# Linear attention feeding a gelu MLP: token quarters in the first group, a later load of k, and batch 2's transposes moved to the crossbar

## The chip, the cores and the metric

The kernel runs on one core of a Trainium2 chip. The metric is the device time of one execution in microseconds (us), as the median of several runs. Times in this document are of that kind unless they are said to be from the profile, which is one execution recorded by the hardware profiler.

The engines are named as the profile names them: PE (TensorE, matrix multiplies, PEld its weight loads), ACT (ScalarE), DVE (VectorE), POOL (GpSimd) and SP (SyncE, which here only issues transfers). Each takes its instructions in the order of the program. DMA stands for the transfers between the memories.

## The reference

```python
def phi(x):
    return np.where(x > 0, x, np.exp(x) - 1.0) + 1.0
q_p, k_p = (phi(q), phi(k))
kv = np.einsum('bhsd,bhse->bhde', k_p, v)
z = np.sum(k_p, axis=2)
num = np.einsum('bhsd,bhde->bhse', q_p, kv)
den = np.einsum('bhsd,bhd->bhs', q_p, z)[..., None] + 1e-06
attn = num / den                                       # 8 batches, 8 heads, 576 tokens, 64 wide
x = attn.transpose(0, 2, 1, 3).reshape(4608, 512)
h = x @ w_in                                           # 512 x 2048
g = 0.5 * h * (1.0 + np.tanh(sqrt(2 / pi) * (h + 0.044715 * h**3)))
out = g @ w_out                                        # 2048 x 512
```

All inputs and the output are float32 in HBM.

## The kernel before

Each batch has 576 tokens: 512 "main" tokens in four chunks of 128, and 64 "rest" tokens. The rests of all batches, 512 tokens, are the ninth group. A group j has a first half (h = x times w_in in 16 blocks of 128 hidden columns, `first_half`, a gelu on each block on ACT) and a second half (16 slots of four matmuls with w_out, `second_half`). The groups run one after the other, and the attention of a later batch is laid between the blocks and slots: `at(ph, j, slot, fn)` hangs a piece of work behind block or slot `slot` of half `ph` of group j. So `(2, 1, 7)` is "second half of group 1, after slot 7". The order of instructions on every engine is the order in which this program writes them.

The attention of a batch is: exps on ACT (`exp_main`; they need another function table than gelu, so a table load stands before and after), phi on DVE (`phi_of`, a line and a minimum), v cast to bf16 on DVE (`cast_v`), the transpose of q (`qt`), kv on PE (`kv_mm`, evacuated by `kv_evac`), the numerator and denominator per chunk on PE (`nab_mm` into n_ps), their quotient x on DVE (`nab_evac`), and the transpose of x into `xts[b]`, which is the right operand of the first half. A transpose is either four PE matmuls against an identity and a copy (`pe_tx`), or one crossbar DMA (`dma_start_transpose`) in SP's queue. Before the change batches 0, 1 and 2 take PE for x, and batches 3 to 7 the crossbar.

SP's queue holds all loads of k, q, v and the weights, and all crossbar transposes. POOL's queue loads the rests. Loads go through six buffers (`pld`), each 1 MB. PSUM has four one-bank buffers (`ps_ho`, for h_ps, o_ps and some transposes) and two two-bank buffers (`ps_a`, for kv, n_ps, transposes, and the wide h_ps of blocks 12 to 15 of groups 0 and 1 and of blocks 4 to 7 of group 0). Some h blocks are begun early on half of their tokens (`first_mm_early`) while the last chunks of x are still being made. For a pair of batches, `plan_rest` transposes the rest's q (`qtr`) and makes its x for `xt_rest`.

Group 0 starts while the weights are still loading: w_in comes in four blocks and w_out in four, each cast to bf16 by POOL (one half of w_out's last by ACT).

Of the kernel before, what the change touches and what calls it, by code (L numbers as in the profile page):

```python
# [8 lines left out]
FP32 = mybir.dt.float32  # L9
# [6 lines left out]
def kernel(  # L16
# [12 lines left out]
    nc = tc.nc  # L29
# [45 lines left out]
    def load_rest_half(src, t, m, s, eng):  # L75
        eng.dma_start(
            out=t[REST * s : REST * (s + 1)],
            in_=src[2 * m + s, :, MAIN:S, :].rearrange("h p d -> p h d"),
        )
# [36 lines left out]
    load_rest_half(k, ld["kr", 0], 0, 0, nc.sync)  # L116
    load_rest_half(v, ld["vr", 0], 0, 0, nc.sync)
    ld["v", 0] = load_main(v, 0, "v_x", nc.sync, parts=2)
    w_st = [load_w_in(0), load_w_in(1, None, slice(0, 256))]
    ld["k", 1] = load_main(k, 1, "k_x", nc.sync)  # L120
    load_rest_half(k, ld["kr", 0], 0, 1, nc.sync)
    load_w_in(1, w_st[1], slice(256, 512))


    ident = const.tile([P, P], BF16, name="ident")
# [244 lines left out]
            kv_mm(0, 2 * h + i, kv_ps, i)  # L370
        kv_evac(0, kv_ps[:, 0:1], h, nc.scalar.copy)
    keep_warm(1)
    for i in range(2):
        cast_w_in_halves(i)
    x_c = []

# [23 lines left out]
    nab0(2)  # L400
    keep_warm(1)
    tx0(1)
    ke1 = exp_main("k", 1)
    kre1 = pe.tile([P, 1, H, D], BF16, name="kr_e")
    exp_rest_half("kr", kre1, 1)
    gelu_table()
    nab0(3)
    tx0(2)
    first_mm_early(0, 0)
    first_mm_early(0, 1)  # L410
    tx0(3)
    first_mm_early(0, 2)
    first_mm_early(0, 3)


    for i in (2, 3):
        w_st.append(load_w_in(i))
        cast_w_in_halves(i)
    phi["k", 1] = phi_of(ld["k", 1], ke1, "k_p")
    phi_rest_half("kr", kre1, 1)  # L420
    wo_st = [load_w_out(0)]
    ld["q", 1] = load_main(q, 1, "q_x", nc.sync, parts=2)
    wo_st += [load_w_out(i) for i in (1, 2)]
    load_rest_half(v, ld["vr", 0], 0, 1, nc.sync)
    ld["v", 1] = load_main(v, 1, "v_x", nc.sync)
    wo_st.append(load_w_out(3))
# [47 lines left out]
            at(*qr_at, lambda: box["qr"]())  # L474
        at(*table_at, gelu_table)

    def plan_attention(b, ph, j, s_kv, s_n):

        box = {}

        def kv(i):
            if i == 0:
                box["kv"] = ps_a.tile([P, 2, 512], FP32, name="kv_ps", tag="a")
            kv_mm(b, i, box["kv"])

        for i in range(NP):
            at(ph, j, s_kv[i], lambda i=i: kv(i))
        at(ph, j, s_kv[3], lambda: kv_evac(b, box["kv"]))

        def nab(c):  # L490
            n_ps = ps_a.tile([P, 2, 512], FP32, name="n_ps", tag="a")
            nab_mm(qts[b][:, c], kvbds[b % 4], n_ps)
            box["x", c] = nab_evac(n_ps)

        def tx(c):
            if c == 0:
                xts[b] = pt.tile([P, NP, MAIN], BF16, name="xt")
            nc.sync.dma_start_transpose(
                out=xts[b][:, :, P * c : P * (c + 1)],
                in_=box["x", c].rearrange("p a t d -> p (a t d)"),  # L500
            )

        for c in range(C):
            at(ph, j, s_n[c], lambda c=c: nab(c))
            at(ph, j, s_n[c], lambda c=c: tx(c))

    def plan_rest(m, j0, j1):
        box = {}
# [21 lines left out]
    def plan_second():  # L530

        b = 1
        box = {}

        def exps():
            box["q"] = pe.tile([P, C, H, D], BF16, name="q_e")
            for s in halves:
                exp_into(box["q"], ld["q", b], s)
            gelu_table()

        def phis():
            phi["q", b] = pphi.tile([P, C, H, D], BF16, name="q_p")
            for s in halves:
                phi_line(phi["q", b], ld["q", b], s)
                phi_min(phi["q", b], box["q"], s)

        def cast_vs():
            cast_vr(0, (1,))
            cast_v(b, nc.vector.tensor_copy)

        def last_w_out():
            cast_w_out_halves(3, (nc.gpsimd.tensor_copy, nc.scalar.copy))
            load_rests(1, (("kr", k), ("vr", v)))
            for s in range(2):
                load_rest_half(q, ld["qr", 0], 0, s, nc.gpsimd)
            load_rests(1, (("qr", q),))

        def kv():
            kv_ps = ps_a.tile([P, 2, 512], FP32, name="kv_ps", tag="a")
            for i in range(NP):  # L560
                kv_mm(b, i, kv_ps)
            kv_evac(b, kv_ps)

        def tq(h):
            if h == 0:
                box["qt"] = pt.tile([P, C, NP, P], BF16, name="qt")
            t_ps = ps_a.tile([P, 4, NP, P], BF16, name="t_ps", tag="a")
            t_q(q_src(b), None, 2 * h, 2, t_ps)
            copy = nc.vector.tensor_copy if h else nc.scalar.copy
            copy(out=box["qt"][:, 2 * h : 2 * h + 2], in_=t_ps[:, 0:2])  # L570

        def nab(c):
            n_ps = ps_a.tile([P, 2, 512], FP32, name="n_ps", tag="a")
            nab_mm(box["qt"][:, c], kvbds[b], n_ps)
            box["x", c] = nab_evac(n_ps)

        def tx(c):
            copy = nc.scalar.copy if c < 2 else nc.vector.tensor_copy
            pe_tx(b, c, box["x", c], c < 2, copy)

        def early(m):
            first_mm_early(1, m)

        at(1, 0, 11, exps)
        at(2, 0, 0, phis)
        at(2, 0, 0, cast_vs)
        for fn, c, slot in (
            (tq, 0, 7), (tq, 1, 7), (lambda c: kv(), 0, 10), (lambda c: last_w_out(), 0, 10),
            (nab, 0, 11), (nab, 1, 12), (nab, 2, 13), (tx, 0, 13), (nab, 3, 14),
            (tx, 1, 14), (tx, 2, 15), (early, 0, 15), (early, 1, 15), (tx, 3, 15),  # L590
            (early, 2, 15),
        ):
            at(2, 0, slot, lambda fn=fn, c=c: fn(c))

    def plan_third():

        b = 2
        box = {}

        def exps():  # L600
            box["k"] = exp_main("k", b)
            box["kr"] = phi_rest("kr", 1)
            box["q"] = exp_main("q", b)
            box["qr"] = phi_rest("qr", 0)
            gelu_table()

        def phis(n):
            phi[n, b] = phi_of(ld[n, b], box[n], n + "_p")

        def cast_vs():  # L610
            cast_v(b, nc.vector.tensor_copy)
            cast_vr(1)

        def qtr():
            qts[b] = pt.tile([P, C, NP, P], BF16, name="qt")
            for c in range(C):
                nc.sync.dma_start_transpose(
                    out=qts[b][:, c],
                    in_=phi["q", b][:, c].rearrange("p h d -> p (h d)"),
                )  # L620

        def kv(i):
            if i == 0:
                box["kv"] = ps_a.tile([P, 2, 512], FP32, name="kv_ps", tag="a")
            kv_mm(b, i, box["kv"])

        def nab(c):
            n_ps = ps_a.tile([P, 2, 512], FP32, name="n_ps", tag="a")
            nab_mm(qts[b][:, c], kvbds[b], n_ps)
            box["x", c] = nab_evac(n_ps)  # L630

        def tx(c):
            copy = nc.scalar.copy if c < 2 else nc.vector.tensor_copy
            pe_tx(b, c, box["x", c], c < 2, copy)

        def early(m):
            first_mm_early(2, m)

        at(1, 1, 10, cast_vs)
        at(1, 1, 11, exps)  # L640
        at(2, 1, 0, lambda: phis("k"))
        at(2, 1, 0, lambda: box["kr"]())
        at(2, 1, 0, lambda: phis("q"))
        at(2, 1, 0, qtr)
        at(1, 2, 3, lambda: box["qr"]())
        for i in range(NP):
            at(2, 1, 8 + i // 2, lambda i=i: kv(i))
        at(2, 1, 9, lambda: kv_evac(b, box["kv"]))
        for fn, c, slot in (
            (nab, 0, 10), (nab, 1, 11), (nab, 2, 12), (nab, 3, 13), (tx, 0, 13),  # L650
            (tx, 1, 14), (tx, 2, 15), (early, 0, 15), (tx, 3, 15), (early, 1, 15),
        ):
            at(2, 1, slot, lambda fn=fn, c=c: fn(c))

    def store(j, t, o_sb):
        if j < B:
# [9 lines left out]
    def first_half(j):  # L666
        gs[j] = pg.tile([P, MM, MAIN], BF16, name="g")
        todo = []
        for m in range(MM):
            if (j, m) in hs:  # L670
                h_ps = hs[j, m]
                first_mm(j, m, h_ps, slice(MAIN // 2, MAIN))
            else:
                if (j < 2 and m >= 12) or (j == 0 and 4 <= m < 8):
                    if m % 2 == 0:
# [74 lines left out]
    plan_prepare(  # L750
        3, (2, 1, 7), (1, 2, 0), None, (1, 2, 1), (2, 1, 15), None, (2, 1, 12)
    )
    plan_attention(3, 1, 2, (7, 8, 9, 10), (12, 13, 14, 15))
    for b in range(4, B):
        j = b - 2
        plan_prepare(
            b, (1, j, 15), (2, j, 1), (2, j, 2), (2, j, 3), (2, j, 5), (2, j, 8), (2, j, 8)
        )
        plan_attention(b, 1, b - 1, (1, 2, 3, 4), (6, 8, 10, 12))
    plan_rest(0, (1, 2, 3), (2, 2, 2))  # L760
    at(2, 1, 7, lambda: box0.__setitem__("qr", phi_rest("qr", 1)))
    at(1, 2, 8, lambda: box0["qr"]())
    plan_rest(1, (2, 2, 8), (1, 3, 14))
    for b in range(4, B):
        at(2, b - 3, 2 if b == 4 else 0, lambda b=b: load_batch(b))
    for m in range(2, 4):
        at(2, 2 * m - 3, 3, lambda m=m: load_rests(m, (("kr", k), ("vr", v))))
        at(1, 2 * m - 2, 9, lambda m=m: load_rests(m, (("qr", q),)))
# [34 lines left out]
```

## Time and profile before

| | us |
|---|---|
| median of 8 runs | 295.92 (294.17 to 297.2) |
| the profiled execution, its device time | 296.36 |
| the profiled execution, its span | 294.6 |
| PE busy in the span | 286.6 |
| ACT busy | 158.9 |
| DVE busy | 113.0 |
| POOL busy | 36.0 |
| DMA, GB/s over the span | 181 |
| first weight matmul (h_ps) | 19.44 |
| first w_out matmul (o_ps) | 35.53 |
| kv of batch 1 starts | 45.99 |
| second half of group 1 starts | 67.8 |
| second half of group 2 starts | 101.1 |

A row of the profile's groups reads: line, engine, operation, what it writes from what it reads, sizes, count, busy time, mean duration in ns, and the idle time ahead of it with what ended it. Rows of a timeline begin with the start and the duration in us; what stands in brackets is the idle time before the row and what ended it. The chain that ended last is followed back from the last instruction to whatever released each step. Matmuls are pipelined: a 128x512 matmul has a duration of 379 ns, but they follow one another every 0.216 us.

### The profile page before, as it was taken

To read this page: it belongs to the slowest core of one execution; us is meant where nothing else is said; L and a number is where in the kernel's file an instruction comes from. 1 tells how busy PE (TensorE), PEld (TensorE's weight loads), DVE (VectorE), ACT (ScalarE), POOL (GpSimd) and SP (SyncE) were. 2 spreads that over 40 slices of the span, in tenths; PEclk is the share of its full clock that TensorE was granted. 3 is DMA by queue.
4 is the path that set the end of the run, shared out by engine and by line. 5 is a ranking of instruction groups with operands and counts; after the bars stand their busy time and mean duration, and the time that the engine had idled before them with its cause. 6 is when DMAs were issued, how large, how long until landed. Compare 5 with 4: busy or idle time off the path is not lost.

```text
span 294.6 us, 4249 instructions
## 1 busy us (share of the span) xinstructions
PE 286.6 (97%) x1698; PEld 148.9 (51%) x1698; DVE 113.0 (38%) x189; ACT 158.9 (54%) x221; POOL 36.0 (12%) x56
## 2 busy tenths in 40 slices
PE   8987999999999999999999999999999999999995
PEld 6873455644565544544454445544554444444443
DVE  3765316336386774256224662543142000000002
ACT  4728953679955682557355925673561066017500
POOL 8044555600004300000000000000000000000000
PEclk9999999999999999999999999999999999999999
DMA  7999999995499989638924798204241110021032
GB/s 241 348 337 336 397 358 388 333 362 187 112 339 274 196 242 328 155 71 263 313 82 73 224 330 127 58 16 126 88 55 36 71 71 2 0 88 54 2 71 71
DMA packets 64259, 53.23 MB, mean 181 GB/s; under 512 B 31728, under 2 KB 57584, under 8 KB 64240
## 3 DMA queue, kind: packets, MB, share of 16 engines
q1 hardware_dynamic: 60816, 41.82, 51.2%
q10 hardware_dynamic: 2464, 8.52, 7.7%
q0 software_dynamic: 960, 2.62, 3.3%
q8 instruction: 13, 0.21, 0.3%
q14 instruction: 6, 0.05, 0.0%
HBM read 36.70 MB, written 9.44 MB: 157 GB/s over the span
## 4 chain that ended last, share of the span: by engine, by line
PE 93%; DMA 3%; DVE 2%; POOL 0%; issue 0%; ACT 0%
PE o_ps L727 41%; PE h_ps L309 40%; PE w_ps L336 4%; DMA w_st<-in_moe_w_in_dram 3%; PE n_ps L261 3%; PE kv_ps L227 3%; PE o_ps L696 1%; PE t_ps L284 1%; DVE kvbd L250 1%; PE kv_ps L234 1%; POOL w_in_sb L149 0%; PE t_ps L344 0%; PE t_ps L255 0%; DVE xt L391 0%; DVE x L273 0%
## 5 line engine op out<-in xcount | busy, mean ns | idle before, releaser
L727 PE MATMUL o_ps<-w_out_sb,g 128*128 128x512 bf16 x560 | 124.7, 379 | 0.0
L309 PE MATMUL h_ps<-xt,w_in_sb 128*128 128x512 bf16 (+1 forms) x548 | 119.9, 365 | 1.8 <-POOL w_in_sb L149 1.7
L684 ACT ACTIVATE g<-h_ps 128x512 bf16<-128x512 f32 x144 | 83.8, 601 | 46.7 <-PE h_ps L309 45.2
L309 PEld LDWEIGHTS <-w_in_sb 128*128 128x128 bf16 x612 | 57.5, 97 | 56.9 <-POOL w_in_sb L149 2.6
L727 PEld LDWEIGHTS <-g 128*128 128x128 bf16 x560 | 54.1, 98 | 62.7 <-issue 0.2
L742 ACT COPY o_sb<-o_ps 128x512 f32<-128x512 f32 x18 | 10.6, 586 | 57.3 <-PE o_ps L727 57.3
L740 DVE COPY o_sb<-o_ps 128x512 f32<-128x512 f32 x17 | 11.7, 689 | 64.5 <-PE o_ps L727 64.5
L273 DVE TENSOR_TENSOR x<-n_ps,r 128x512 bf16<-128x512 f32 x36 | 24.9, 692 | 1.2
L250 DVE CAST kvbd<-kv_ps 64x260 bf16<-64x260 f32 (+1 forms) x16 | 6.6, 410 | 39.0 <-PE kv_ps L234 38.9
L168 ACT ACTIVATE k_e<-k_x 128x2048 bf16<-128x2048 f32 (+1 forms) x9 | 15.5, 1721 | 6.3 <-DMA k_x<-in_k_dram 6.2
L168 ACT ACTIVATE q_e<-q_x 128x2048 bf16<-128x2048 f32 (+1 forms) x10 | 15.6, 1559 | 2.4 <-DMA q_x<-in_q_dram 2.3
L271 DVE RECIPROCAL r<-n_ps 128x8 f32<-128x8 f32 x36 | 7.4, 206 | 24.0 <-PE n_ps L261 24.0
L185 DVE TENSOR_TENSOR k_p<-k_p,k_e 128x2048 bf16<-128x2048 bf16 (+1 forms) x9 | 10.5, 1171 | 13.9 <-ACT k_e L168 13.7
L336 PE MATMUL w_ps<-warm 128*128 128x252 bf16 x94 | 13.5, 308 | 1.1 <-DVE warm L127 1.1
L309 PE MATMUL h_ps<-xt_rest,w_in_sb 128*128 128x512 bf16 x64 | 14.0, 379 | 0.0
L261 PEld LDWEIGHTS <-qt 128*128 128x128 bf16 x128 | 9.7, 98 | 7.9 <-issue 1.0
L179 DVE TENSOR_SCALAR q_p<-q_x 128x2048 bf16<-128x2048 f32 (+1 forms) x10 | 10.7, 1067 | 7.2 <-DMA q_x<-in_q_dram 7.2
L211 DVE CAST vp<-v_x 128x2048 bf16<-128x2048 f32 (+1 forms) x9 | 9.3, 1046 | 10.5 <-DMA v_x<-in_v_dram 10.5
L261 PE MATMUL n_ps<-kvbd,qt 128*128 128x130 bf16 x128 | 12.7, 221 | 0.5 <-ACT kvbd L250 0.2
L227 PEld LDWEIGHTS <-k_p 128*128 128x128 bf16 x128 | 9.6, 96 | 6.1 <-DVE vp L211 0.9
L227 PE MATMUL kv_ps<-vp,k_p 128*128 128x130 bf16 x128 | 11.8, 220 | 0.4 <-DVE vp L211 0.4
L179 DVE TENSOR_SCALAR k_p<-k_x 128x2048 bf16<-128x2048 f32 (+1 forms) x9 | 9.9, 1103 | 5.2 <-DMA k_x<-in_k_dram 5.1
(52 smaller groups left out, 139.1 us busy)
## 6 DMA issues: line engine op xcount, KB each, us to landing
out_dram<-o_sb ACTq DMA_DIRECT2D x16, 512.0 KB, 4.9
k_x<-in_k_dram SPq DMA_DIRECT2D x7, 1024.0 KB, 6.0
v_x<-in_v_dram SPq DMA_DIRECT2D x7, 1024.0 KB, 11.9
q_x<-in_q_dram SPq DMA_DIRECT2D x6, 1024.0 KB, 8.6
w_st<-in_moe_w_out_dram SPq DMA_DIRECT2D x4, 1024.0 KB, 11.3
w_st<-in_moe_w_in_dram SPq DMA_DIRECT2D x3, 1024.0 KB, 9.9
q_x<-in_q_dram SPq DMA_DIRECT2D x4, 512.0 KB, 9.6
k_x<-in_k_dram SPq DMA_DIRECT2D x2, 512.0 KB, 4.1
```

The lines of the kernel that those rows point to most:

```text
L168: nc.scalar.activation(e[:, :, hs, :].rearrange("p c h d -> p h c d"), by_chunk(x[:, hs]), AF.Exp)
L179: nc.vector.tensor_scalar(xp[:, :, hs, :].rearrange("p c h d -> p h c d"), by_chunk(x[:, hs]), 1.0, 1.0, op0=ALU.add, op1=ALU.max,)
L185: nc.vector.tensor_tensor(xp[:, :, hs, :], xp[:, :, hs, :], e[:, :, hs, :], op=ALU.min)
L227: nc.tensor.matmul(dst, lhsT=kp[:, c, P * i : P * (i + 1)], rhs=vps[b % 2][:, 2 * i : 2 * i + 2, c, :], start=(c == 0), stop=False,)
L261: nc.tensor.matmul(n_ps[rows, i // 2, 2 * E * (i % 2) : 2 * E * (i % 2) + 2 * E], lhsT=qt_c[:, i, rows], rhs=kvbd[:, i, :], skip_group_che ...
L273: nc.vector.tensor_tensor(x, n_v[:, :, :, 0:D], r[:, :, :, None].to_broadcast([P, 2, 4, D]), op=ALU.mult,)
L309: nc.tensor.matmul(h_ps[:, tok], lhsT=w_in_sb[:, c, P * m : P * (m + 1)], rhs=xt[:, c, tok], start=(c == 0), stop=(c == KM - 1), skip_grou ...
L336: nc.tensor.matmul(w_ps[:, 0:252], lhsT=warm[:, 0:P], rhs=warm)
L684: nc.scalar.activation(gs[j][:, i, :], ps, AF.Gelu_apprx_tanh)
L727: nc.tensor.matmul(o_pss[t], lhsT=g[:, m, P * t : P * (t + 1)], rhs=w_out_sb[:, m, :], start=(m == 0), stop=(m == MM - 1),)
L740: nc.vector.tensor_copy(dst, o_ps)
L742: nc.scalar.copy(dst, o_ps)
```

## The change

It has three parts.

In the first group, blocks 0 to 3 of h are computed by token quarters instead of halves, each quarter behind the transpose that yields it. The early load of k of batch 1, which stood between the halves of w_in's second block, goes behind w_in, w_out's first two blocks and q; its exp and phi join those of q behind block 11 (`plan_second`), and w_in's second block is loaded in one piece. The transposes of batch 1's q move from slot 7 to slot 8.

Batch 2's x is transposed by the crossbar (`plan_third`). Its kv moves from slots 8 and 9 to slot 5 of group 1's second half, its n_ps from slots 10 to 13 to slots 7 to 10, q is handled before k, and four instead of two h blocks are begun early, behind slot 15.

Batch 3's n_ps and x move from the first half of group 2 (blocks 12 to 15) to its second half (slots 1 to 4). Batch 4's phi, casts and q transposes, the loads of batches 4 and 5, and the first two rests move to later slots.

```diff
-    w_st = [load_w_in(0), load_w_in(1, None, slice(0, 256))]
-    ld["k", 1] = load_main(k, 1, "k_x", nc.sync)
-    load_rest_half(k, ld["kr", 0], 0, 1, nc.sync)
-    load_w_in(1, w_st[1], slice(256, 512))
+    w_st = [load_w_in(i) for i in range(3)]
...
-    for i in range(2):
+    for i in range(3):
         cast_w_in_halves(i)
...
-    ke1 = exp_main("k", 1)
-    kre1 = pe.tile([P, 1, H, D], BF16, name="kr_e")
-    exp_rest_half("kr", kre1, 1)
     gelu_table()
+    quarters = [slice(P * c, P * (c + 1)) for c in range(C)]
+
+    def first_mm_quarter(c, ms):
+        for m in ms:
+            if c == 0:
+                hs[0, m] = ps_ho.tile([P, MAIN], FP32, name="h_ps", tag="ho")
+            first_mm(0, m, hs[0, m], quarters[c])
+
     nab0(3)
+    first_mm_quarter(0, (0, 1))
     tx0(2)
-    first_mm_early(0, 0)
-    first_mm_early(0, 1)
+    first_mm_quarter(0, (2, 3))
+    first_mm_quarter(1, (0, 1))
     tx0(3)
-    first_mm_early(0, 2)
-    first_mm_early(0, 3)
-    for i in (2, 3):
-        w_st.append(load_w_in(i))
-        cast_w_in_halves(i)
-    phi["k", 1] = phi_of(ld["k", 1], ke1, "k_p")
-    phi_rest_half("kr", kre1, 1)
+    first_mm_quarter(1, (2, 3))
+    first_mm_quarter(2, range(4))
+    w_st.append(load_w_in(3))
+    cast_w_in_halves(3)
     wo_st = [load_w_out(0)]
     ld["q", 1] = load_main(q, 1, "q_x", nc.sync, parts=2)
-    wo_st += [load_w_out(i) for i in (1, 2)]
+    wo_st.append(load_w_out(1))
+    ld["k", 1] = load_main(k, 1, "k_x", nc.sync)
+    load_rest_half(k, ld["kr", 0], 0, 1, nc.sync)
+    wo_st.append(load_w_out(2))
...
-    def plan_attention(b, ph, j, s_kv, s_n):
+    def plan_attention(b, ph, j, s_kv, s_n, ph_n=1):
...
-            at(ph, j, s_n[c], lambda c=c: nab(c))
-            at(ph, j, s_n[c], lambda c=c: tx(c))
+            at(ph_n, j, s_n[c], lambda c=c: nab(c))
+            at(ph_n, j, s_n[c], lambda c=c: tx(c))
...
+            box["k"] = exp_main("k", b)
+            box["kr"] = pe.tile([P, 1, H, D], BF16, name="kr_e")
+            exp_rest_half("kr", box["kr"], 1)
             gelu_table()
...
+            phi["k", b] = phi_of(ld["k", b], box["k"], "k_p")
+            phi_rest_half("kr", box["kr"], 1)
...
-            (tq, 0, 7), (tq, 1, 7), (lambda c: kv(), 0, 10), (lambda c: last_w_out(), 0, 10),
+            (tq, 0, 8), (tq, 1, 8), (lambda c: kv(), 0, 10), (lambda c: last_w_out(), 0, 10),
...
         def exps():
+            box["q"] = exp_main("q", b)
             box["k"] = exp_main("k", b)
             box["kr"] = phi_rest("kr", 1)
-            box["q"] = exp_main("q", b)
-            box["qr"] = phi_rest("qr", 0)
             gelu_table()
...
         def tx(c):
-            copy = nc.scalar.copy if c < 2 else nc.vector.tensor_copy
-            pe_tx(b, c, box["x", c], c < 2, copy)
+            if c == 0:
+                xts[b] = pt.tile([P, NP, MAIN], BF16, name="xt")
+            nc.sync.dma_start_transpose(
+                out=xts[b][:, :, P * c : P * (c + 1)],
+                in_=box["x", c].rearrange("p a t d -> p (a t d)"),
+            )
...
+        at(2, 1, 0, lambda: phis("q"))
+        at(2, 1, 0, qtr)
         at(2, 1, 0, lambda: phis("k"))
         at(2, 1, 0, lambda: box["kr"]())
-        at(2, 1, 0, lambda: phis("q"))
-        at(2, 1, 0, qtr)
-        at(1, 2, 3, lambda: box["qr"]())
         for i in range(NP):
-            at(2, 1, 8 + i // 2, lambda i=i: kv(i))
-        at(2, 1, 9, lambda: kv_evac(b, box["kv"]))
-        for fn, c, slot in (
-            (nab, 0, 10), (nab, 1, 11), (nab, 2, 12), (nab, 3, 13), (tx, 0, 13),
-            (tx, 1, 14), (tx, 2, 15), (early, 0, 15), (tx, 3, 15), (early, 1, 15),
-        ):
-            at(2, 1, slot, lambda fn=fn, c=c: fn(c))
+            at(2, 1, 5, lambda i=i: kv(i))
+        at(2, 1, 5, lambda: kv_evac(b, box["kv"]))
+        for c, slot in enumerate((7, 8, 9, 10)):
+            at(2, 1, slot, lambda c=c: nab(c))
+            at(2, 1, slot, lambda c=c: tx(c))
+        for m in range(4):
+            at(2, 1, 15, lambda m=m: first_mm_early(2, m))
...
-    plan_attention(3, 1, 2, (7, 8, 9, 10), (12, 13, 14, 15))
+    plan_attention(3, 1, 2, (7, 8, 9, 10), (1, 2, 3, 4), 2)
     for b in range(4, B):
         j = b - 2
-        plan_prepare(
-            b, (1, j, 15), (2, j, 1), (2, j, 2), (2, j, 3), (2, j, 5), (2, j, 8), (2, j, 8)
-        )
+        slots = (6, 7, 8, 5, 9, 8) if b == 4 else (1, 2, 3, 5, 8, 8)
+        plan_prepare(b, (1, j, 15), *((2, j, s) for s in slots))
         plan_attention(b, 1, b - 1, (1, 2, 3, 4), (6, 8, 10, 12))
-    plan_rest(0, (1, 2, 3), (2, 2, 2))
-    at(2, 1, 7, lambda: box0.__setitem__("qr", phi_rest("qr", 1)))
-    at(1, 2, 8, lambda: box0["qr"]())
-    plan_rest(1, (2, 2, 8), (1, 3, 14))
+    plan_rest(0, (1, 2, 3), (2, 2, 9))
+    for m in range(2):
+        at(2, 1, 7, lambda m=m: box0.__setitem__(m, phi_rest("qr", m)))
+        at(1, 2, 2 + 6 * m, lambda m=m: box0[m]())
+    plan_rest(1, (2, 2, 10), (1, 3, 14))
     for b in range(4, B):
-        at(2, b - 3, 2 if b == 4 else 0, lambda b=b: load_batch(b))
+        at(2, b - 3, {4: 12, 5: 9}.get(b, 0), lambda b=b: load_batch(b))
```

## The prediction, made before the result was known

> **What bounds the kernel now.** I read the page's busy times first, then the chain that ended last, then the timeline at the places that the change touches, last the landing times that the trace gives for single transfers.
>
> The page (busy time; groups, whose last columns are busy us and mean ns of one):
>
> ```profile
> PE 286.6 (97%) x1698; PEld 148.9 (51%) x1698; DVE 113.0 (38%) x189; ACT 158.9 (54%) x221; POOL 36.0 (12%) x56
> ...
> L727 PE MATMUL o_ps<-w_out_sb,g 128*128 128x512 bf16 x560 | 124.7, 379 | 0.0
> ```
>
> TensorE (PE) works 286.6 of 294.6 us. The stretches say where it does not: 25.88 of 27.75 us busy from 18.40 to 46.15, and at most 0.3 us idle in each later stretch up to 291.3. So the change can win by taking PE work away, or in the 1.9 us before 46; everything else must show as a new wait.
>
> The chain that ended last, in order of time (start us, us, what), at the two places where it leaves PE:
>
> ```profile
> 18.40 9.06 DMA w_st<-in_moe_w_in_dram
> 27.51 1.05 POOL w_in_sb L149
> 28.61 7.08 PE h_ps L309 x32
> ...
> 83.43 0.22 PE t_ps L284 x4
> ...
> 85.18 0.24 PE t_ps L284 x4
> 85.44 0.44 DVE xt L391
> 85.92 6.21 PE h_ps L309 x32
> ```
>
> Above: w_in's blocks come late (PE's idle gaps are 0.56 and 1.10 us). Below: batch 2's x is transposed by PE, four times, and PE then waits for the last copy.
>
> The timeline where the first group ends, and SyncE's (SP's) queue in group 2's second half:
>
> ```profile
> 32.89 1.28 ACT L168 ACT_TABLE_LOAD   x1
> 41.40 2.23 POOL L156 CAST w_out_sb<-w_st 128x1024 bf16<-128x1024 f32 x2 [1.41 <-DMA w_st<-in_moe_w_out_dram]
> 44.53 1.23 DVE L211 CAST vp<-v_x 128x2048 bf16<-128x2048 f32 x1 [1.80 <-DMA v_x<-in_v_dram]
> 45.81 0.40 PEld L227 LDWEIGHTS <-k_p 128*128 128x128 bf16 x4 [0.15 <-DVE vp L211]
> ```
>
> ```profile
> 105.31 1.51 SPq L67 DMA_DIRECT2D v_x<-in_v_dram  x1
> 107.75 4.75 SPq L522 DMA_TRANSPOSE xt_rest<-x  x1
> ```
>
> Batch 1's kv starts as soon as v of batch 1 is landed and cast: DMA and PE arrive there together. The second fence matters below: by the trace that v landed 11.9 us after its issue, at 117.2, and the crossbar transpose issued behind it 10.0 us after its own, at 117.8.
>
> **What the Trainium skill says.** "DMA: Bandwidth & Descriptors", section "Queues, rings and completion order": each DMA engine takes the descriptors of one ring in order. The trace agrees: a transpose issued behind three loads lands 0.6 us after the last of them; with nothing ahead (qtr at 119.5 and 120.9) it takes 2.3 to 2.6 us. Same page, "Anatomy of one DMA": a DMA's semaphore wait is on the issuing sequencer, so an SP transfer that waits holds up all behind it. "TensorE: Matmul & The Clock Gate", "Architectural detail: the array is 16x 32x32": ACT and DVE are strictly first in, first out. In the trace the gelus of blocks 12 to 15 stand from 32.87 to 37.70 behind two table loads (1.28 each) and q's exps. "VectorE: DVE Perf Modes", "The three transpose paths", prices a 128x128 crossbar transpose at 1.3 us against 0.39 on TensorE; here four of them, as one 128x512 instruction, cost SP 1.2 to 1.3 us and TensorE 0.23 us.
>
> **Part 1, batch 2's x by the crossbar.** Four groups of transposes at 0.23 go: 0.92 us of PE. Their copies (two on ACT by 0.59, two on DVE by 0.43) go too; they lie beside PE's matmuls but for the last, the 0.44 of the chain. In their place come four transposes in SP's queue, some 5 us ahead of batch 4's loads (part 3). Measured another way: from 67.81 to 92.13 (second half of group 1 and eight blocks of group 2) PE took 24.32 us. The rest of its work is 64 matmuls by 0.2158 (13.81), four kv by 0.29 (1.16), four n_ps by 0.23 (0.93) and 32 matmuls (6.91), in all 22.81. So **1.5 us** go, 0.6 of them waits, if the new arrangement hides. kv moves to slot 5, ready for PE at 72.99. ACT: table to 66.3, q exp 68.2, k 70.0, kr 70.6, table 71.8, so gelus 12 and 13 free the PSUM buffer at 72.85; DVE gives kr_p at 72.6. Margin 0.1 to 0.4: cost 0; ACT has lost the first rest's q exp (0.61) ahead of these gelus, which is what makes it fit, and if it fits not, PE waits by what is missing, 0.5 at most. q's transposes issue at 69.5 and land by about 76; n_ps at slots 7 to 10 begins at 75.9. The x transposes are issued at 77.2, 78.4, 79.7 and 81.0 and land 2.4 later, by 83.4; PE asks for the first two at 83.7 and for the others at 85.4. Cover 2 us, cost 0; without it each us late costs one.
>
> **Part 2, the first group.** Quarters: 64 matmuls by 58 ns (as kv's 4 in 0.23) instead of 32 by 109: +0.2 us, and 0.3 waiting at 20.0 for the cast of w_in's second half block, which ends at 20.28. Blocks 4 on begin at 23.8 (before: 23.2). k of batch 1 (3 us of queue) is now behind, so w_in blocks 1 to 3 land near 21, 23.6 and 26.3 instead of 24.5, 27.5 and 30.1; with casts of 2.03 all are ahead of PE, which runs 12 blocks by 0.863 to 34.15 (before 35.7). The two gaps go. But the same bytes, k included, still precede w_out block 2 (landed 41.3) and v (44.5). PE has eight slots of 0.863 done at 41.05 and waits for w_out block 2's cast at 42.4; then three slots and q's transposes (0.92) end at 46.0, as before. Joining w_in block 1's halves and fewer stalls of 256-byte pieces ahead may bring the transfers 0 to 0.7 us forward: I take **0.25**, bounds -0.4 and +0.9.
>
> k's exp now stands ahead of gelus 12 to 15. With k landing near 37: exp 1.91, kr 0.6, table 1.28, four gelus 2.06, done at 42.9; q's transposes need the second buffer by 43.8. Cover 0.9 us: cost 0. Without that cover the order is: gelus late, wide PSUM buffers late, q's transposes, slots 9 and 10, kv. POOL's casts keep their number and order of blocks.
>
> **Part 3, batch 3's n_ps half a group later, loads later.** n_ps by four 0.23 only moves. Batch 4's loads are issued at 82.0 instead of 78.1; v came 16.0 us after the first issue, so 96.5 to 98, and q's transposes of batch 3 behind it at 98.5 to 102.3. PE asks from 100.1 to 103.4: about 1 us of cover, cost 0.
>
> Now group 2's second half, which starts at T. DVE has batch 3's x until T+6.6, then batch 4's q and k (2.47 each), kr 0.86, v and vr 2.04, qr 0.86 and the rest's x 0.9: T+16.2. SP issues xt_rest then (1.25), and behind it batch 5's loads at T+17.5 (before: T+3.0), and behind them the two qtr transposes. v lands 13.1 to 13.3 us after the first issue (batches 5 to 7), T+30.2 to T+30.8; qtr of the second rest pair is second behind it, +0.9: T+31.1 to T+31.7. PE asks for it in slot 14 of the next first half: 15.2 for this half with its n_ps, and 15.05 as in before (115.41 to 130.46), T+30.25. **New wait: 1.1 us**, bounds 0 (the store ahead of the loads has drained by then, v 1.3 early) and 4 (a landing after 16 us, as batch 4's). Before, the same qtr landed 7 us early. Queued behind it on PE is all of group 3.
>
> **Sum.** 1.5 + 0.25 - 1.1 = 0.65 us less: span 293.95. The profiled execution took 296.36 (1.76 around its span), so 295.7 for that one; it lies 0.44 above the median, 295.92, from which 0.65 leaves **295.3**. About 0.5% (1.5 us) is what a measurement of this kernel can tell from no change.
>
> **Rivals.** (A, the forecast, 46%) as summed; own range 294.5 to 296.2. (B, 26%) qtr is not late: 1.5 to 1.9 us gained, 294.2. For it: the margin at stake is 1.1 of 31 us. Against: every transpose of before that was issued behind loads landed after v. (C, 6%) the transfers really come earlier and v of batch 1 lands at 43 or sooner: 1 us more, 293.5. Against: the bytes are the same, and DMA is busy throughout. (D, slower, 14%) k of batch 1 lands late and ACT stands: at its place w_out block 1 landed at 37.9. From 37.9 on, each us delays gelus, PSUM, q's transposes and kv by one; at 40.5 it is +2.6, and 297.9 with the rest. It ends above 295.92 from 38.6 on. (E, 8%) another stall behind loads (q of batch 3) or in the tight slot 5: 296.5 to 298.
>
> **Chances and range.** Faster by over 0.5%: most of B and C, a little of A: 0.28. Slower by over 0.5%: D's larger half and most of E, 0.17. Within: 0.55. To leave no more than 2 in 10 out, the range reaches from C's 293.5 to the middle of D and E, 297.4; the likeliest case alone is 294.5 to 296.2.
>
> **What would show it.** Part 1: no t_ps by PE between 67 and 92 and that stretch 1.5 us shorter. Part 2: no PE wait on w_in's cast after 24, instead a wait of about 1 us near 41 to 42 for w_out's third block, and kv of batch 1 within 0.5 us of 46. Part 3: PE idle about 1 us before the n_ps from qtr, near 128, ended by a DMA. Wrong if that gap is missing, if kv starts before 45 or after 47, or if PE waits at slot 5 or for q of batch 3.

## The result, and the profile after

The changed kernel took 300.9 us in the median of 11 runs (298.94 to 304.03), against 295.24 us for the kernel before, measured beside it (32 runs, 294.17 to 297.2). The ratio is 1.0183, 95% interval 1.0157 to 1.0208: it is slower by 1.8%, and outside the range of the forecast. The profiled execution took 300.26 us with a span of 298.5. Of the experiments below, the profile of the eighth fell into a disturbed execution (306.08 us) and is not read.

The page of the kernel after (busy time; the granted clock of TensorE in 40 slices of the span; two of the groups, with busy us, mean ns of one, and the idle time ahead of them):

```profile
PE 288.1 (97%) x1722; PEld 150.5 (50%) x1722; DVE 113.0 (38%) x187; ACT 157.9 (53%) x219; POOL 36.7 (12%) x56
...
PEclk9999999999999779999999999999999999999999
...
L734 PE MATMUL o_ps<-w_out_sb,g 128*128 128x512 bf16 x560 | 127.4, 384 | 0.1
...
L258 PE MATMUL n_ps<-kvbd,qt 128*128 128x130 bf16 x128 | 13.4, 229 | 4.5 <-DMA qt<-q_p 4.2
```

PE has one new idle stretch: 4.2 us ahead of an n_ps, ended by a crossbar transpose of q. The clock falls in the slices behind it, so that o_ps, the same 560 matmuls as before, are busy for 127.4 us, not 124.7.

The chain of the kernel after, in order of time, at the two places shown of the kernel before:

```profile
10.43 10.90 DMA w_st<-in_moe_w_in_dram
...
43.94 0.23 PE kv_ps L224 x4
...
81.66 3.98 PE h_ps L306 x35
85.64 16.91 DMA qt<-q_p
102.55 0.05 issue
102.60 0.61 PE n_ps L258 x4
103.22 1.71 PE o_ps L734 x4
104.92 0.43 PE n_ps L258 x4
105.36 1.71 PE o_ps L734 x4
```

The step over DVE's copy of batch 2's x is gone, as intended. In its place the chain leaves PE for 16.91 us: the first transpose of batch 3's q, issued at 85.64, landed at 102.55. Behind it four o_ps take 1.71 us instead of 0.86.

A sum by stages finds where the time is. I take the starts of the first matmuls of each half from the timelines, counted from kv of batch 1:

| us | before | after | difference |
|---|---|---|---|
| start of batch 1's kv | 45.99 | 43.78 | -2.21 |
| from there to group 1's second half | 21.66 | 21.66 | 0.00 |
| group 1's second half | 16.93 | 16.06 | -0.87 |
| group 2's first half | 16.39 | 15.01 | -1.38 |
| group 2's second half | 14.28 | 22.35 | +8.07 |
| group 3's first half | 16.38 | 16.38 | 0.00 |
| from there to the end of the span | 162.97 | 163.26 | +0.29 |
| span | 294.6 | 298.5 | +3.9 |

Batch 3's four n_ps are 0.94 of the -1.38 and of the +8.07 (the half without a stall takes 15.22 in experiment 1, against 14.28 before): they only moved. So part 1 won 1.31 us, and the stall cost 7.13. Of these PE was idle for 4.2; the slow clock took the other 2.9 (from the chain: two groups of four o_ps 0.85 longer each, a third 0.47, three n_ps together 0.8). The 0.29 lies behind the last matmul, from whose end to the end of the span it is 3.58 us before and 3.88 after; no run looked into it. The first row varies between executions (last section); with the early gain that the medians show for part 2, 0.4 us (experiment 4), the same table gives 5.7 us of loss. The ratio gives 5.4, the medians 5.7 (6.0 and 6.3 in experiment 7).

The transfers around the stall. The first fence is the timeline of the kernel before, POOL's rest loads and SP's queue; the second that of the kernel after:

```profile
92.74 1.36 POOL L76 DMA_DIRECT2D q_r<-in_q_dram  x2 [34.40 <-DVE qr_p L185]
...
78.12 0.58 SPq L67 DMA_DIRECT2D k_x<-in_k_dram  x1
...
79.42 1.63 SPq L67 DMA_DIRECT2D v_x<-in_v_dram  x1
88.39 5.74 SPq L463 DMA_TRANSPOSE qt<-q_p  x4
```

```profile
80.26 0.58 SPq L67 DMA_DIRECT2D k_x<-in_k_dram  x1
...
81.55 3.99 SPq L67 DMA_DIRECT2D v_x<-in_v_dram  x1
...
88.41 1.36 POOL L76 DMA_DIRECT2D q_r<-in_q_dram  x2 [32.95 <-DVE qr_p L182]
```

Two things moved towards each other: batch 4's loads, and POOL's eight rest loads, which wait until DVE has used up the first rest's q. POOL's began 14.6 us behind batch 4's first load before, and 8.2 us behind it after. Counted from the start of group 1's second half, batch 4's loads come 4.35 us later, which is most of the difference; POOL's come 2.1 earlier, 0.9 of it because that half is shorter and 1.25 because the phi hangs one slot earlier. Before, v of batch 4 landed at 94.09, when POOL's loads had hardly begun. After, POOL's loads begin 12.1 us before v has landed.

Windows of 4 us of the kernel after (columns: busy us and count of PE, PEld, DVE, ACT and POOL; granted clock; share of DMA busy; GB/s):

```profile
92.00:96.00 4.00, 4.00 (x24) 1.96 (x23) 0.85 (x2) 2.54 (x5) 1.81 (x3) 1.00 1.96 282
96.00:100.00 4.00, 2.40 (x12) 0.88 (x9) 0.00 (x0) 3.70 (x4) 0.00 (x0) 1.00 0.47 50
100.00:104.00 4.00, 1.40 (x7) 0.85 (x8) 0.71 (x2) 3.37 (x4) 0.00 (x0) 0.68 1.01 181
104.00:108.00 4.00, 4.00 (x17) 1.89 (x16) 1.90 (x6) 0.00 (x0) 0.00 (x0) 0.50 0.59 118
```

From 96 to 100 the DMA engines moved only 50 GB/s, although v, most of POOL's loads and the transposes were all outstanding. V landed at 100.55, 20.3 us after the batch's first issue (16.0 before), and the four transposes at 102.55, 104.55, 104.77 and 105.12.

### The profile page after: what moved, and what is told of

It reads as the page before. It is cut to its first block, busy times and chain, and to the rows that moved or that the text cites. A ratio compares the mean times of both kernels' runs of the same rounds, so it can differ in the third digit from the quotient of the medians.

```text
span 298.5 us, 4302 instructions
## 1 busy us (share of the span) xinstructions
PE 288.1 (97%) x1722; PEld 150.5 (50%) x1722; DVE 113.0 (38%) x187; ACT 157.9 (53%) x219; POOL 36.7 (12%) x56
## 4 chain that ended last, share of the span: by engine, by line
PE 79%; DMA 13%; SPq 5%; POOL 1%; DVE 1%; issue 0%
PE o_ps L734 38%; PE h_ps L306 34%; DMA qt<-q_p 6%; DMA w_st<-in_moe_w_in_dram 4%; DMA w_st<-in_moe_w_out_dram 3%; PE n_ps L258 3%; SPq L76 2%; SPq L67 2%; PE kv_ps L224 2%; PE o_ps L703 1%; POOL w_in_sb L146 1%; SPq L90 1%; PE kv_ps L231 0%; POOL w_out_sb L153 0%; PE t_ps L281 0%
## 5 line engine op out<-in xcount | busy, mean ns | idle before, releaser
L734 PE MATMUL o_ps<-w_out_sb,g 128*128 128x512 bf16 x560 | 127.4, 384 | 0.1
L306 PE MATMUL h_ps<-xt,w_in_sb 128*128 128x512 bf16 (+2 forms) x588 | 119.0, 351 | 0.1
L734 PEld LDWEIGHTS <-g 128*128 128x128 bf16 x560 | 54.7, 99 | 63.6 <-issue 2.0
L306 PEld LDWEIGHTS <-w_in_sb 128*128 128x128 bf16 x652 | 59.2, 98 | 54.3 <-issue 0.3
L258 PE MATMUL n_ps<-kvbd,qt 128*128 128x130 bf16 x128 | 13.4, 229 | 4.5 <-DMA qt<-q_p 4.2
L176 DVE TENSOR_SCALAR q_p<-q_x 128x2048 bf16<-128x2048 f32 (+1 forms) x10 | 11.6, 1156 | 7.6 <-DMA q_x<-in_q_dram 7.4
L182 DVE TENSOR_TENSOR q_p<-q_p,q_e 128x2048 bf16<-128x2048 bf16 (+1 forms) x10 | 10.1, 1012 | 5.7 <-ACT q_e L165 5.1
## 6 DMA issues: line engine op xcount, KB each, us to landing
v_x<-in_v_dram SPq DMA_DIRECT2D x7, 1024.0 KB, 11.8
```

The source lines that it names most:

```text
L176: nc.vector.tensor_scalar(xp[:, :, hs, :].rearrange("p c h d -> p h c d"), by_chunk(x[:, hs]), 1.0, 1.0, op0=ALU.add, op1=ALU.max,)
L182: nc.vector.tensor_tensor(xp[:, :, hs, :], xp[:, :, hs, :], e[:, :, hs, :], op=ALU.min)
L258: nc.tensor.matmul(n_ps[rows, i // 2, 2 * E * (i % 2) : 2 * E * (i % 2) + 2 * E], lhsT=qt_c[:, i, rows], rhs=kvbd[:, i, :], skip_group_che ...
L306: nc.tensor.matmul(h_ps[:, tok], lhsT=w_in_sb[:, c, P * m : P * (m + 1)], rhs=xt[:, c, tok], start=(c == 0), stop=(c == KM - 1), skip_grou ...
L734: nc.tensor.matmul(o_pss[t], lhsT=g[:, m, P * t : P * (t + 1)], rhs=w_out_sb[:, m, :], start=(m == 0), stop=(m == MM - 1),)
```

## The experiments

The theory after the result: the transposes are late because they stand in SP's queue behind 3 MB of loads (place), and these loads are late because POOL's rest loads meet them (collision). Rivals: the place alone is enough; or the first group's new order of loads is at fault. A side question is how much of the loss is the clock.

**1. Batch 4's loads behind the transposes.** It takes the place away and leaves POOL's loads where they are.

```diff
-        at(2, b - 3, {4: 12, 5: 9}.get(b, 0), lambda b=b: load_batch(b))
+        at(*{4: (1, 2, 4), 5: (2, 2, 9)}.get(b, (2, b - 3, 0)), lambda b=b: load_batch(b))
```

> The changed kernel with batch 4's three loads moved in SP's queue from ahead of batch 3's q transposes to behind them and behind the first rest's (slot 4 of group 2's first half). Theory F (the transposes are late because they stand behind 3 MB of loads in one ring): they land within 3 us of their issue, by 92, PE does not wait for them at 98, the clock stays full, and the time falls by 5 to 7.5 us from the changed kernel's 300.9, to 293.5 to 296; what it may lose is up to 2.5 us at the second rest's q transpose near 126, since batch 4 and so batch 5's loads come later. Theory R (POOL's rest loads in 256-byte pieces, which start near 88, hold up any crossbar transpose that meets them): the transposes are issued from 85.6 on, meet them just the same, and part of the wait stays; 297 to 300.

Measured: 298.46 us, ratio 1.0107 (1.008 to 1.0134). The transposes were issued from 84.39 and landed from 87.72 to 92.41, and no PE wait for them is left; group 2's second half takes 15.22 us. But group 3's first half takes 21.09 instead of 16.38. The longest of this kernel's waits of PE (total us, times, longest), and after it its chain:

```profile
PE h_ps L306 <- DVE o_sb L747: 2.7, 1, 2.7
...
```

```profile
90.86 11.81 DMA k_x<-in_k_dram
...
104.04 0.93 ACT k_e L165
...
115.79 0.69 DVE x L270
116.48 0.61 DVE o_sb L747
...
117.13 1.02 PE h_ps L306 x4
```

Now batch 4's k is late: issued at 90.86 amid POOL's loads, it lands 11.8 us later. Its exp is late on ACT, the phis are late on DVE, and behind them in DVE's order stands the copy that frees a PSUM buffer. So the place decides which load is waited for, but moving it only moves the stall. The time lies in the range of the second theory, but not for its reason: POOL's loads began at 88.74, while the transposes were landing, and these took only 2.4 to 4.2 us from issue to landing.

**2. The first rest's phi and x later.** It takes the collision away and leaves the place.

```diff
-    plan_rest(0, (1, 2, 3), (2, 2, 9))
+    plan_rest(0, (1, 2, 13), (2, 2, 9))
...
-        at(1, 2, 2 + 6 * m, lambda m=m: box0[m]())
+        at(1, 2, 11 + m, lambda m=m: box0[m]())
```

> The changed kernel with the first rest's phi moved on DVE behind batch 3's kv (slots 11 and 12 instead of 2 and 8), so that the buffer which POOL's eight rest loads wait for comes free near 94 instead of 88; SP's queue keeps its order up to the rest's own transpose. Theory F alone: v of batch 4 still lands near 100, PE waits 3 to 5 us, 299 to 301. Theory R: v lands by 96, the first q transpose of batch 3 by 97.5, PE waits less than 1 us, the clock stays full, 293.5 to 296.

Measured: 295.17 us, ratio 0.9981 (0.996 to 1.0002). The timeline of this kernel:

```profile
82.07 0.58 SPq L67 DMA_DIRECT2D k_x<-in_k_dram  x1
...
87.63 10.02 SPq L466 DMA_TRANSPOSE qt<-q_p  x4
...
96.08 1.36 POOL L76 DMA_DIRECT2D q_r<-in_q_dram  x2 [38.65 <-DVE qr_p L182]
```

The loads and transposes stand in the same order as in the changed kernel, but POOL's loads begin at 96.08, 14.0 us behind batch 4's first load. (The edit also moves the first rest's own transpose and x; neither stands ahead of v or of batch 3's transposes in SP's queue.) V lands at 97.50, 15.4 us after the first issue, the transposes from 98.03 to 101.28, and PE waits for none of them. That is 1.5 and 0.5 us later than the second theory had v and the first transpose, in a profile whose loads of batch 4 began 1.8 us later than in the changed kernel's; the time is in its range. The place alone is therefore not enough; the meeting with POOL's loads is what makes the stall. Two windows of this kernel, to set against those of 96 to 104 above:

```profile
96.00:100.00 4.00, 4.00 (x20) 1.81 (x19) 0.82 (x3) 3.18 (x5) 3.92 (x6) 1.00 1.11 208
100.00:104.00 4.00, 4.00 (x31) 2.30 (x30) 3.25 (x8) 3.99 (x4) 1.48 (x3) 1.00 1.04 216
```

With the stall gone, the wait that the prediction had priced appears. PE waits for qtr, 1.6 us by its own row and 2.1 by that of its weight loads:

```profile
PE n_ps L258 <- DMA qtr<-qr_p: 1.6, 1, 1.6
```

Group 3's first half is 18.05 us here, 1.67 longer than before. This profile is the slowest of the 20 executions (296.66 us), so the wait may be shorter in most of them. In the changed kernel this wait was only 0.4 us on the weight loads, because the stall had put PE behind.

**3. and 8. Filler matmuls in the stall.** 24 matmuls on a tile of zeros, whose result nothing reads, before the first n_ps of batch 3. They keep TensorE busy for 2.7 us in which it would wait. The kernel was run twice, on two chips.

```diff
+    at(2, 2, 1, lambda: keep_warm(12))
     plan_attention(3, 1, 2, (7, 8, 9, 10), (1, 2, 3, 4), 2)
```

> The changed kernel with 24 matmuls on zeros (252 columns, 2.5 us, no part of the result) set on PE between slot 1 of group 2's second half and batch 3's first n_ps, where PE waits 4.7 us. Theory C (the gap halves the granted clock, and that costs a further 2.9 us after the wait): the wait for the transposes ends at the same time, the clock stays at 1.0, the time falls by 2 to 3 us to 298 to 299. If the clock costs nothing the time stays at 300.9 or rises by up to 0.5.

> The changed kernel with the 24 matmuls on zeros in the gap (no part of the result), once more. In the first run of it the clock stayed full (0.999) but the time was 301.22 over four runs, on a chip without the changed kernel beside it. Theory C (the lowered clock costs about 2 us after the wait): 1.5 to 2.5 us below the changed kernel of this call. Else: within 0.7 us of it.

Measured: 301.22 us, ratio 1.0235 (1.0161 to 1.0309), then 300.67, ratio 1.0161 (1.0129 to 1.0193). The changed kernel beside the second of them took 302.04 (experiment 7). In the profile of the first (windows, same columns) the clock stays up:

```profile
100.00:104.00 4.00, 3.65 (x29) 2.64 (x27) 0.00 (x0) 3.99 (x4) 0.00 (x0) 1.00 0.61 93
104.00:108.00 4.00, 2.34 (x16) 1.18 (x17) 1.49 (x4) 2.03 (x2) 0.00 (x0) 1.00 1.07 199
```

Group 2's second half takes 20.17 us instead of 22.35, with the first n_ps 5.8 us after the half's start instead of 6.1. So of the 2.2 us, 0.3 are a shorter stall and about 1.9 the clock. That is less than the 2.9 above, in part because PE at full speed waits another 0.7 for the second transpose. In the half that follows 0.43 is given back to the wait for qtr. For the whole time the two series disagree (0.3 above the first median of the changed kernel, 1.4 below the second, where 1.5 to 3 below was expected); what the clock costs is read from this one profile's stage, not from the medians.

**4. Part 2 alone**: the kernel before, with the new first group.

```diff
+    w_st = [load_w_in(i) for i in range(3)]
...
+    first_mm_quarter(2, range(4))
...
+    ld["k", 1] = load_main(k, 1, "k_x", nc.sync)
```

> The kernel before with the change in the first group alone (token quarters, k of batch 1 behind, w_in's second block in one piece, q's transposes in slot 8); batches 2 to 5 as before. From the profile of the changed kernel, in which kv of batch 1 starts 2.2 us earlier: 2.2 us faster than before, 293, with v of batch 1 landing near 42. From the prediction's step (the same bytes are ahead of v, so 0.25): 295. A loss would show that the rest of the change made room for it.

Measured: 295.58 us, ratio 0.9985 (0.9964 to 1.0006). Batch 1's kv starts at 44.51, and from there to the end of the span it takes 248.7 us; the kernel before takes 248.6. The first group isn't the cause of the loss. Its gain, about 0.4 us, can't be told from none, since the interval holds 1.

**5. and 9. Both waits out.** Experiment 2, and batch 5's loads behind the two qtr transposes. Run on two chips.

```diff
-        at(2, b - 3, {4: 12, 5: 9}.get(b, 0), lambda b=b: load_batch(b))
+        at(2, b - 3, {4: 12, 5: 11}.get(b, 0), lambda b=b: load_batch(b))
```

> The kernel of the run with the rests later (0.9981 of before; its profile shows PE 2.1 us in wait for the second rest's q transpose near 128), with batch 5's loads moved from slot 9 to slot 11 of group 2's second half, so that both rest transposes stand ahead of these 3 MB in SP's queue. If that wait is a place in the queue: it goes, the rest's transposes land within 6 us of their issue, and the ratio falls by 2.1 of 295.6 to 0.991 (0.989 to 0.994), 293.0. Rival: something else is late behind it (batch 5's own k, or DVE): 0.996 to 1.0.

> The kernel of the fifth experiment again, in one call with that of the sixth, to rank them. If the first-group part is worth the 0.4 us that it showed alone, this one is 0.3 to 0.5 us below the other, at 293.1 to 294.7; if it is worth nothing once the later waits are out, or harmful, this one is level or up to 1.2 us above it, as the medians of the two calls stood (294.7 against 293.52). No wait of TensorE for transposes of q or of the rests' q in either theory.

Measured: 294.7 us, ratio 0.9966 (0.9945 to 0.9987), and 294.71, ratio 0.9965 (0.9945 to 0.9984). The qtr are issued at 115.03 and 116.82 and land 2.4 and 3.2 us later; group 3's first half is 16.37 us. PE's waits of the first of these kernels, all of them:

```profile
PE w_ps L333 <- DVE warm L124: 1.1, 1, 1.1
PE o_ps L734 <- POOL w_out_sb L153: 0.7, 1, 0.7
PE kv_ps L224 <- DVE vp L208: 0.5, 1, 0.5
PE t_ps L281 <- DVE x L270: 0.4, 1, 0.4
PE n_ps L258 <- ACT kvbd L247: 0.3, 1, 0.3
```

None is for a transpose by the crossbar. This version beats both kernels: it is 7.3 us below the changed one on the same chip (experiment 7), and 0.35% below the one before. But the expected ratio, 0.991, was missed: by the ratios it gains only 0.4 us on experiment 2, where the stage is 1.67 us shorter. No run settles how much of the qtr wait most executions of experiment 2 had.

**6. and 10. The same without part 2**: parts 1 and 3 with both waits out, and the old first group.

```diff
-    w_st = [load_w_in(i) for i in range(3)]
+    w_st = [load_w_in(0), load_w_in(1, None, slice(0, 256))]
+    ld["k", 1] = load_main(k, 1, "k_x", nc.sync)
...
```

> The same kernel with the first group as in the kernel before, so parts 1 and 3 of the change alone with both transposes' waits taken out. From the prediction's step for part 1 (1.5 us of PE work and waits between the start of group 1's second half and group 2's eighth block): 0.995 of before, 294.1. If part 2 carries the gain instead: 0.998 to 1.0, and the run before it would owe more than 1 us to the first group.

> The kernel of the sixth experiment again. If its 293.52 was the rule, ratio to before 0.990 to 0.994 and 293 to 294; if its six runs were a lucky draw, it lies with the fifth's at 0.995 to 0.998.

Measured: 293.52 us, ratio 0.9919 (0.9889 to 0.9949), from 6 runs; then 295.28, ratio 0.9973 (0.9953 to 0.9994), from 22. The intervals do not overlap, and the stages agree, so the first was most likely a lucky draw of few runs: an interval from one chip need not hold what another chip gives. Beside experiment 9, on the same chip, the first group is worth 0.2 us by the ratios and 0.6 by the medians, again within the noise. The stages agree in all four profiles of experiments 5, 6, 9 and 10: from batch 1's kv to the end 247.5 to 247.6 us, 1.0 to 1.1 less than before. That is what part 1 with a harmless part 3 brings: the 1.31 of the table less some 0.25 by which the stretch behind the last matmul is longer here too.

**7. The changed kernel again**, beside these.

> The changed kernel unaltered, beside the next one on one chip: 1.018 of before, 300 to 302, a PE wait of 4 to 6 us for batch 3's first q transpose and the clock halved behind it.

Measured: 302.04 us, ratio 1.0204 (1.0162 to 1.0247). PE's wait was 4.1 us, v landed at 100.76 and the first transpose at 103.10; group 2's second half took 22.08 us. The stall is no accident of one profile.

## Why the prediction was wrong

**The step that failed is in part 3**: "v came 16.0 us after the first issue, so 96.5 to 98, and q's transposes of batch 3 behind it at 98.5 to 102.3 [...] about 1 us of cover, cost 0". V came 20.3 us after the first issue, at 100.55, and the first transpose at 102.55. The step took a duration measured under one load of the DMA engines over to another. It followed SP's queue and not POOL's: the change puts batch 4's loads later and the first rest's phi earlier, and the step did not ask what the eight loads that this phi releases would then meet. POOL's loads came 8.2 us behind batch 4's first load instead of 14.6, and v lost 4.3 us. Experiment 2, with the distance back at 14.0, meets the numbers of the step (15.4 us; 98.03 to 101.28).

A section of the Trainium skill that the prediction used for the order within a ring says more that bears on this: "DMA: Bandwidth & Descriptors", section "Queues, rings and completion order", has each DMA engine alternate between the queues that have work, a packet at a time. The traces agree in kind: with POOL's queue active SP's loads take 20.3 us, without it 15.4. But sharing is not the whole of it, since the engines at the same time moved only 50 GB/s; no run here takes that apart (last section).

**The price of the rival that happened** (E, which names a stall behind loads for q of batch 3) was wrong too: 296.5 to 298 allows for 2 us, and it cost 7.1. It counted no loss of clock, about 2 to 3 us of it, and no load that is itself late.

**Part 1** was right in kind and 0.2 too high: 1.31 us went from the two halves, against 1.5. Batch 2's x transposes are hidden as said: from the start of group 1's second half, at 65.60 in the chain, to the first kv of batch 3 at 88.61 PE is busy for all of 23.01 us, against the 22.81 of the sum. Of the missing 0.2, 0.16 lies at the tight slot 5, where the first four kv matmuls take 0.39 us instead of 0.23.

**Part 2** is not contradicted, and not confirmed: 0.25 said, about 0.4 measured (ratio 0.9985, with an interval that holds 1). Its sign for a failure, kv before 45, is met by the profile of the changed kernel (43.78) without a failure of the size, since that time varies. Its inner step, a wait of about 1 us for w_out's third block near 41 to 42, is met in kind: in seven of the eight profiles with the new first group PE waits 0.3 to 0.75 us for that cast, between 40.5 and 42.9. Only the profile of the changed kernel above is without it: its cast begins at 38.98 and lets o_ps go on at 40.30. K of batch 1 was no hazard (rival D): its phi on DVE begins at 35.74.

**The wait for qtr** was right in cause, and its size was too low in the one profile that shows it: 1.1 us said, 1.67 in the stage of experiment 2, within the bounds 0 to 4. The ratios of experiments 2 and 5 differ by less, 0.4 us. In the changed kernel the larger stall hides it.

With the collision out, the sum of the prediction, 0.2% below the kernel before, stands against 0.19% measured in experiment 2. That the totals agree is partly luck: the interval (0.996 to 1.0002) holds anything from no gain to 1.2 us, and in the profile of that run the parts are other than forecast, 1.31 us won, 1.67 lost to qtr and 0.3 behind the last matmul.

## What to carry to other kernels

When a piece of work moves, ask on every queue what the buffer it frees releases, and when: here SP's loads moved one way and the phi that releases POOL's loads the other, and the two queues met. A landing time read from a trace holds for the traffic of that moment only; where PE waits for crossbar transposes that stand behind loads, give them a stretch in which no other queue starts loads, or more cover than one such meeting costs. And price a wait of several us with the clock that is lost behind it.

## What the runs showed of the hardware

**Loads and transposes that meet.** POOL's eight rest loads of 128 KB landed 5.7 to 11.4 us after their issue in the changed kernel, and 3.6 to 5.5 in the kernel before. For 4 us the DMA engines moved 50 GB/s, against 208 in experiment 2 in the same window. By single microseconds the changed kernel's engines moved 325 to 408 GB/s from 86 to 94, and only 23 to 34 from 96 to 99 (34 to 50 from 97 to 100 in experiment 7). A like dip is there without the stall, but for one microsecond: 40 GB/s from 93 to 94 in the kernel before, 68 from 96 to 97 in experiment 2. So the bytes of POOL's loads alone do not make the delay: their 1 MB is worth 2.8 us at the 380 GB/s of these eight windows (an estimate), and v came 4.9 later than in experiment 2. What the engines wait for in the long dip no run shows.

**The clock after a gap.** One-microsecond windows of the kernel after (same columns as above):

```profile
98.00:99.00 1.00, 0.40 (x2) 0.00 (x0) 0.00 (x0) 0.99 (x2) 0.00 (x0) 1.00 0.17 34
...
101.00:102.00 1.00, 0.00 (x0) 0.00 (x0) 0.00 (x0) 1.00 (x2) 0.00 (x0) 0.74 1.36 205
102.00:103.00 1.00, 0.40 (x4) 0.41 (x5) 0.00 (x0) 1.00 (x2) 0.00 (x0) 0.50 0.97 238
...
108.00:109.00 1.00, 1.00 (x8) 0.58 (x7) 0.69 (x1) 0.00 (x0) 0.00 (x0) 0.85 0.25 52
```

And of experiment 1, whose gap was 2.67 us, from 114.46 to 117.13:

```profile
118.00:119.00 1.00, 1.00 (x9) 0.55 (x8) 0.00 (x0) 1.00 (x3) 0.00 (x0) 0.71 1.10 365
119.00:120.00 1.00, 1.00 (x5) 0.45 (x4) 0.00 (x0) 0.12 (x1) 0.00 (x0) 0.50 0.91 233
...
121.00:122.00 1.00, 1.00 (x5) 0.33 (x3) 0.00 (x0) 0.00 (x0) 0.00 (x0) 0.58 1.06 322
```

After 4.2 us of idleness the clock is at half for some 6.8 us, of which about one still lies in the gap. In experiment 7, after 4.1 us, it is 6.8 us again. After 2.67 us it falls too, 1.3 us after PE has resumed, for about 3.4 us. The Trainium skill, "TensorE: Matmul & The Clock Gate", "Part 1: The HAM clock gate", says that the clock is halved after an idle window of about 3.4 us that runs freely, and comes back after as long a busy one. The half rate agrees, and 3.4 and 6.8 us are once and twice that length. But an idle window is not needed here: the 3.4 us ahead of the falls held only 3.1, 2.7 (experiment 7) and 2.1 us (experiment 1) of idleness, and the measurement decides. Gaps of 1.3 us and less with the filler, and of 1.6 us in experiment 2, left the clock at 1.00.

**The first stage varies.** Batch 1's kv started between 43.78 and 46.44 in eight profiles with the new first group (mean 44.8), and at 45.16, 45.67 and 45.99 in the three with the old one (mean 45.6). The 2.2 us that the changed kernel's one profile gained there was mostly this; only stages counted from a fixed event could be compared between single profiles.
